# A fused attention-and-experts kernel: the beginning rebuilt (S summed in PSUM, first features on TensorE, divisors inverted once a column, chunks of up to 512 columns)

## Chip, cores and metric

The kernel runs on one core of a Trainium2 chip. The metric is the device time of one execution in microseconds (us), the median of several. Executions with a profile also give a span, from the first to the last instruction; in those used here the time is 1.75 to 2.1 us more than the span.

## The reference, cut

Polysketch attention is followed by four small experts, all weighted by gates.

```python
# q, k, v: (4 batches, 4 heads, 1088 positions, 32); S1, S2: (8, 32), double precision
def phi(x):                       # 64 features a position: products of two sketches of 8
    a, b = S1 @ x, S2 @ x
    return outer(a, b)
q_p, k_p = phi(q), phi(k)
kv  = sum over positions of k_p (x) v          # 64 x 32 for each batch and head
z   = sum over positions of k_p                # 64
num = q_p . kv;   den = q_p . z + 1e-6
x   = (num / den), as 4352 rows of 128 columns (4 heads x 32)
p   = domain_probs / (sum + 1e-9)              # (4352, 4)
out = sum over e of p[:, e] * (relu(x @ w1[e]) @ w2[e])   # w1: 128 x 1024, w2: 1024 x 128
```

## The kernel before

The experts' work runs transposed: 128 rows of x or of hidden units on the partitions, positions along the columns. Every product is done in two halves of 64 output columns of the array:

```python
def product(out, weights, moving, **flags):
    for r in (slice(0, 64), slice(64, P)):
        nc.tensor.matmul(out[r, :], weights[:, r], moving, **flags)
```

The positions go in 14 chunks of 128 to 384 columns. For each chunk there are 32 steps: `hp` = w1 part times xT, an eviction on VectorE (maximum with 0, times the gate, into `hid`), and `acc` += w2 part times `hid`. The attention of later chunks is cut into pieces; one piece is issued a step, so that it lies beside the experts. The first chunk has nothing to lie beside, and that is `start()`:

```python
kn[0] = load_rows(k, 0, "kn")
vn[0] = load_v(0, (nc.sync, nc.scalar))     # ten loads, six of them issued by ScalarE
qn[0] = load_rows(q, 0, "qn")
load_weights(0)
nc.vector.memset(warm[:, :], 0.0)
nc.scalar.activation(warm[:, 0:1], warm[:, 1:2], ACTF.Identity)   # behind ScalarE's loads
for _ in range(13):                          # the warm-up multiplications, on `warm`
    nc.tensor.matmul(wp[:, :], warm[:, 0:P], warm[:, :], start=True, stop=True)
...
def start():
    # kT; gates; q transposed; kf = k times both parts of S (high and low, side by side)
    # fs = high part copied by ScalarE, low part added by VectorE; kp = products of features
    # (VectorE and GpSimd); kv = sums over positions
    # q: one product, then shuffles, an add and multiplications on VectorE
...
def queries(b, ch):      # its end, for every chunk
    for p in range(2):
        product(nd[p][:, 0:n], kvzs[b][:, p, :], qp[p][:, 0:n], start=True, stop=True)
    # half of nd[p] holds numerators, the other half denominators, 32 equal rows a head
    for p in range(2):
        nc.scalar.activation(den[64*p : 64*p+64, 0:n], nd[p][64-64*p : 128-64*p, 0:n],
                             ACTF.Identity, bias=eps[64*p : 64*p+64, :])
    for s in range(0, n, P):
        nc.vector.reciprocal(den[:, s : s+w], den[:, s : s+w])
    for p in range(2):
        nc.vector.tensor_tensor(out=xT[r, 0:n], in0=nd[p][r, 0:n], in1=den[r, 0:n], op=ALU.mult)
```

The gates are normed on VectorE and GpSimd, transposed, stored to DRAM, and loaded again, broadcast to all partitions, one load a chunk.

Of the kernel before, what the change touches and what calls it, by code (L numbers as in the profile page):

```python
# [22 lines left out]
def kernel(  # L23
# [19 lines left out]

    nc = tc.nc

    P = 128
    B, H, S, D = q.shape
    E, DM, F = w1.shape
    R = 8
    G = S // 32  # L50
# [3 lines left out]
    NK = E * FB  # L54
    CW = 384
    GE = 160
    LA = 2
    WIDTHS = [[192, 256, 320, 320], [384, 384, 320], [384, 384, 320], [384, 384, 192, 128]]
    assert all(sum(w) == S for w in WIDTHS)

    cpool = ctx.enter_context(tc.tile_pool(name="const", bufs=1))
    lpool = ctx.enter_context(tc.tile_pool(name="loads", bufs=2))
    apool = ctx.enter_context(tc.tile_pool(name="attn", bufs=2))
    mpool = ctx.enter_context(tc.tile_pool(name="moe", bufs=2))
    ps_h = ctx.enter_context(tc.tile_pool(name="ps_h", bufs=2, space=bass.MemoryType.PSUM))
    ps_o = ctx.enter_context(tc.tile_pool(name="ps_o", bufs=2, space=bass.MemoryType.PSUM))
    ps_f = ctx.enter_context(tc.tile_pool(name="ps_f", bufs=2, space=bass.MemoryType.PSUM))
    ps_n = ctx.enter_context(tc.tile_pool(name="ps_n", bufs=2, space=bass.MemoryType.PSUM))
    dram = ctx.enter_context(tc.tile_pool(name="dram", bufs=1, space=bass.MemoryType.DRAM))
    ctx.enter_context(tc.manual_schedule())  # L70


    def load_rows(src, b, name):
        t = lpool.tile([P, S], F32, tag=name, name=name)
        nc.sync.dma_start(t[:, :], bass.AP(src.tensor, src.offset + b * H * S * D, [[G * D, P], [1, G * D]]))
        return t

    def load_v(b, engines):
        t = lpool.tile([P, H * NT * D], F32, tag="vn", name="vn")
        base = v.offset + b * H * S * D  # L80
        for r in range(2):
            for a in range(4):
                engines[r].dma_start(
                    _ap(t, 32 * a, 32, 512 * r, [[P, H], [1, P]]),
                    bass.AP(v.tensor, base + (16 * r + 4 * a) * D, [[G * D, 32], [S * D, H], [1, 4 * D]]),
                )
        for a in range(2):
            engines[1].dma_start(
                _ap(t, 32 * a, 32, 1024, [[D, H], [1, D]]),
                bass.AP(v.tensor, base + (32 + a) * D, [[G * D, 32], [S * D, H], [1, D]]),  # L90
            )
        return t

    kn, qn, vn = {}, {}, {}

# [16 lines left out]
    vn[0] = load_v(0, (nc.sync, nc.scalar))  # L112
    qn[0] = load_rows(q, 0, "qn")
    load_weights(0)
# [4 lines left out]
    nc.scalar.activation(warm[:, 0:1], warm[:, 1:2], ACTF.Identity)  # L119

    own2 = cpool.tile([P, 2], F32, name="own2")
    eps = cpool.tile([P, 1], F32, name="eps")
    sk = cpool.tile([P, P], F32, name="sk")
    sq = cpool.tile([P, P], F32, name="sq")
    nc.gpsimd.memset(sk[:, :], 0.0)
    nc.gpsimd.memset(sq[:, :], 0.0)
    nc.gpsimd.memset(own2[:, :], 0.0)
    nc.gpsimd.memset(eps[:, :], 1e-6)
# [4 lines left out]
    vx = []  # L133
    for i in range(2):
        vx.append(cpool.tile([P, NT, H, D + 1], F32, name=f"vx{i}"))
        nc.gpsimd.memset(vx[i][:, :, :, D : D + 1], 1.0)

    def product(out, weights, moving, **flags):

        for r in (slice(0, 64), slice(64, P)):  # L140
            nc.tensor.matmul(out[r, :], weights[:, r], moving, **flags)  # L141


    for _ in range(13):
        wp = ps_h.tile([P, 512], F32, tag="h", name="wp")
        nc.tensor.matmul(wp[:, :], warm[:, 0:P], warm[:, :], start=True, stop=True)  # L146

# [42 lines left out]

    R2 = 2 * R
    for h in range(H):
        (nc.vector.tensor_copy if h % 2 else nc.scalar.copy)(
            _ap(sk, 32 * h, 32, R2 * h, [[H * R2, 2], [1, R2]]), _ap(s_T, 0, 32, 0, [[D, 2], [1, R2]])
        )
        nc.gpsimd.tensor_copy(_ap(sq, 32 * h, 32, 32 * h, [[R2, 2], [1, R2]]), _ap(s_T, 0, 32, 0, [[D, 2], [1, R2]]))

    mask_lo = [R2 + l % R2 for l in range(32)]
# [13 lines left out]

    def make_gates():
# [5 lines left out]
    def store_gates():  # L219
        nc.vector.transpose(pt[:, :], pn[:, :])  # L220
        for b in range(B):
            nc.sync.dma_start(
# [4 lines left out]
    gate, xT, c0 = {}, {}, {}  # L227
    for b in range(B):
        for ch, n in enumerate(WIDTHS[b]):
            c0[b, ch] = sum(WIDTHS[b][:ch])  # L230

    def load_gate(b, ch):
        n = WIDTHS[b][ch]
        gt = mpool.tile([P, CW * E], F32, tag="gate", bufs=3, name="gate")
        nc.sync.dma_start(gt[:, 0 : n * E], gates[b, c0[b, ch] * E : (c0[b, ch] + n) * E].partition_broadcast(P))
        gate[b, ch] = gt

    ready = []
    WP = 2 * (D + 1)
# [3 lines left out]
    fss, kps = {}, {}  # L243

    def key_turn(b, r):
        if r < 2:
            nc.vector.transpose(
                _ap(kT, 0, P, 512 * r, [[32, 4], [P, 4], [1, 32]]),
                _ap(kn[b], 0, P, 512 * r, [[P, 4], [32, 4], [1, 32]]),
            )  # L250
        else:
            nc.vector.transpose(kT[:, 1024:S], kn[b][:, 1024:S])

    def value_copy(b, copy):
        ve = vx[b % 2]
        for r in range(2):
            copy(
                ve[:, 4 * r : 4 * r + 4, :, 0:D].rearrange("p t h d -> p h t d"),
                _ap(vn[b], 0, P, 512 * r, [[P, H], [D, 4], [1, D]]),
            )  # L260
        copy(ve[0:64, 8, :, 0:D], _ap(vn[b], 0, 64, 1024, [[D, H], [1, D]]))

    def key_project(b, gi):

        t0, n = FG[gi]
        if gi == 0:
            fss[b] = apool.tile([P, NT, H * R2], F32, tag="fs", name="fs")
            kps[b] = apool.tile([P, NT, 2, P], F32, tag="kp", name="kp")
        kf = ps_f.tile([P, 512], F32, tag="f", name="kf")
        for t in range(n):  # L270
            product(
                kf[:, P * t : P * t + P], kT[:, P * (t0 + t) : P * (t0 + t + 1)], sk[:, :], start=True, stop=True
            )
        nc.scalar.copy(fss[b][:, t0 : t0 + n, :], _ap(kf, 0, P, 0, [[P, n], [1, H * R2]]))  # L274
        return kf

    def key_add(b, gi, kf):
        t0, n = FG[gi]
        nc.vector.tensor_tensor(  # L279
            out=fss[b][:, t0 : t0 + n, :],  # L280
            in0=_ap(kf, 0, P, H * R2, [[P, n], [1, H * R2]]),
            in1=fss[b][:, t0 : t0 + n, :],
            op=ALU.add,
        )

    def key_product(b, t0, n, h, x, eng):
        eng.tensor_tensor(  # L287
            out=_ap(kps[b], 0, P, 256 * t0 + P * (h // 2) + 64 * x + 32 * (h % 2), [[256, n], [R, 4], [1, R]]),
            in0=_ap(fss[b], 0, P, 64 * t0 + R2 * h + 4 * x, [[64, n], [1, 4], [0, R]]),
            in1=_ap(fss[b], 0, P, 64 * t0 + R2 * h + R, [[64, n], [0, 4], [1, R]]),  # L290
# [3 lines left out]
    def key_sum(b, p, kv, heads):  # L294

        ve = vx[b % 2]
        for t in range(NT):
            n = min(P, S - P * t)
            product(
                kv[:, 256 * p : 256 * p + heads.stop * (D + 1) - heads.start * (D + 1)],  # L300
                kps[b][0:n, t, p, :],
                ve[0:n, t, heads].rearrange("p h d -> p (h d)"),
# [4 lines left out]
    def key_divide(b, kv, first_pair, step):  # L307


        kvz = apool.tile([P, 2, P], F32, tag="kvz", name="kvz")  # L310
        for off, by_pair, src, by_d in ((0, 192, 0, 1), (64, 64, D, 0)):
            nc.vector.tensor_tensor(  # L312
                out=_ap(kvz, 0, P, off, [[by_pair, 2], [D, 2], [1, D]]),
                in0=_ap(kv, 0, P, first_pair + src, [[step, 2], [D + 1, 2], [by_d, D]]),
# [5 lines left out]
    def keys(b):  # L320
# [3 lines left out]
        kf = [key_project(b, 0)]  # L324
        yield
        kf.append(key_project(b, 1))
        yield
        key_add(b, 0, kf[0])
        yield
        key_add(b, 1, kf[1])  # L330
        kf.append(key_project(b, 2))
        yield
        value_copy(b, nc.scalar.copy)
        key_add(b, 2, kf[2])
        for t0, n in ((0, 4), (4, 5)):
            for h in range(H):
                for x in range(2):
                    key_product(b, t0, n, h, x, nc.gpsimd)
        yield
        for _ in range(8):  # L340
            yield
        kv = ps_f.tile([P, 512], F32, tag="f", name="kv")
        for p in range(2):
            key_sum(b, p, kv, slice(2 * p, 2 * p + 2))
            yield
        key_divide(b, kv, 0, 256)
        yield

    kvzs = {}

    def queries(b, ch):
        n, g0 = WIDTHS[b][ch], c0[b, ch] // 32
        qT = apool.tile([P, CW], F32, tag="qT", name="qT")
        nc.vector.transpose(qT[:, 0:n], qn[b][:, 32 * g0 : 32 * g0 + n])  # L354
        yield
        yield
        qc = ps_f.tile([P, 512], F32, tag="f", name="qc")
        product(qc[:, 0:n], sq[:, :], qT[:, 0:n], start=True, stop=True)
        yield
        qf = apool.tile([P, CW], F32, tag="qf", name="qf")  # L360
# [4 lines left out]
        qb = apool.tile([P, CW], F32, tag="qb", name="qb")  # L365
        nc.vector.stream_shuffle(in_=qf[:, 0:n], out=qb[:, 0:n], mask=mask_b)
        yield
        qp = [apool.tile([P, CW], F32, tag=f"qp{p}", name=f"qp{p}") for p in range(2)]
        for x in range(2):
            qa = apool.tile([P, CW], F32, tag="qa", name="qa")  # L370
            nc.vector.stream_shuffle(in_=qf[:, 0:n], out=qa[:, 0:n], mask=mask_a[x])  # L371
            yield
            for p in range(2):
                nc.vector.tensor_tensor(  # L374
                    out=qp[p][64 * x : 64 * x + 64, 0:n],
                    in0=qa[64 * p : 64 * p + 64, 0:n],
# [193 lines left out]
```

## Time and profile before

| | before |
|---|---|
| time, median of 4 | 537.77 us (536.57 to 537.88) |
| span of the profiled execution | 534.7 us |
| TensorE busy | 518.1 us (97%) |
| VectorE busy | 333.5 us (62%) |
| first product of the experts (`hp`) | at 27.09 us |
| last product of the experts ends | at 531.1 us |

The prediction below shows the chain.

In the first 9 us TensorE does nothing, then 4.3 us of warm-up alone, then 13.8 us in which it and VectorE take turns. This is what the change is after. (The clock column reads 1.00 in the second line, although the first seven multiplications of the warm-up came every 0.43 us and the later ones every 0.21. The trace's record of the clock begins at 11.70 us only, and the column counts what lies before as full.)

### The profile page before, as it was taken

What the parts mean: (1) busy time and instruction counts of PE and PEld (TensorE: products, weight loads), DVE (VectorE), ACT (ScalarE), POOL (GpSimd) and SP (SyncE); (2) the same over time, 40 slices, a digit from 0 to 9 for tenths busy, and PEclk for the clock granted to TensorE, in tenths of its full rate; (3) what the DMA queues carried; (4) which work ended last, traced back from release to release, by engine and by line L of the source; (5) the groups of instructions that cost most, each with busy time, mean ns of one, the idle gap of its engine ahead of it and who ended that gap; (6) DMA issues with size and microseconds to landing.
All of it is one profiled execution on the core that took longest, in us unless ns stands there. A gap on an engine that the chain in (4) does not pass through costs nothing.

```text
span 534.7 us, 9910 instructions
## 1 busy us (share of the span) xinstructions
PE 518.1 (97%) x4197; PEld 287.0 (54%) x4197; DVE 333.5 (62%) x788; ACT 25.3 (5%) x56; POOL 26.1 (5%) x80
## 2 busy tenths in 40 slices
PE   3799999999999999999999999999999999999997
PEld 1677776555554445544554445454555444444896
DVE  3878874777647645367866754447875664654554
ACT  1210000000000001000000000100000000000000
POOL 2240000000000004000000000400000000000000
PEclk9999999999999999999999999999999999999999
DMA  7492502002015002000202001100301000100100
GB/s 209 109 276 103 157 28 71 0 1 73 1 49 139 2 0 77 1 1 8 67 2 63 1 0 23 53 1 0 75 1 31 12 1 10 26 1 2 16 9 8
DMA packets 32893, 22.82 MB, mean 43 GB/s; under 512 B 21200, under 2 KB 29520, under 8 KB 32848
## 3 DMA queue, kind: packets, MB, share of 16 engines
q1 hardware_dynamic: 31536, 21.78, 14.7%
q8 instruction: 33, 0.54, 0.4%
q10 hardware_dynamic: 1312, 0.40, 0.4%
q14 instruction: 12, 0.10, 0.1%
HBM read 19.87 MB, written 2.31 MB: 41 GB/s over the span
## 4 chain that ended last, share of the span: by engine, by line
PE 95%; DVE 2%; DMA 1%; issue 1%; ACT 0%; SPq 0%; DVEq 0%; ACTq 0%
PE hp L141 44%; PE acc L141 44%; PE nd L141 3%; PE kv L141 1%; PE qc L141 1%; PE kf L141 1%; PE wp L146 1%; DMA kn<-in_k_dram 1%; DVE kp L287 1%; DVE den L399 0%; DMA vn<-in_v_dram 0%; DVE qp L374 0%; DVE fs L279 0%; DVE hid L492 0%; ACT den L389 0%
## 5 line engine op out<-in xcount | busy, mean ns | idle before, releaser
L492 DVE SCALAR_TENSOR_TENSOR hid<-hp,gate 128x384 f32<-128x384 f32 (+4 forms) x448 | 213.4, 476 | 185.4 <-PE hp L141 176.8
L141 PE MATMUL hp<-xT,w_sb 128*64 128x384 f32 (+4 forms) x1792 | 311.5, 426 | 1.2 <-DVE xT L404 1.0
L141 PE MATMUL acc<-hid,w_sb 128*64 128x384 f32 (+4 forms) x1792 | 311.0, 425 | 0.0
L141 PEld LDWEIGHTS acc<-hid,w_sb 128*64 128x64 f32 x1792 | 128.6, 137 | 106.9 <-issue 68.7
L141 PEld LDWEIGHTS hp<-xT,w_sb 128*64 128x64 f32 x1792 | 126.8, 137 | 106.0 <-issue 62.6
L287 POOL TENSOR_TENSOR kp<-fs 128x128 f32<-128x128 f32 (+1 forms) x56 | 22.6, 443 | 310.9 <-DVE fs L279 310.9
L399 DVE RECIPROCAL den<-den 128x128 f32<-128x128 f32 (+1 forms) x37 | 32.3, 876 | 0.2 <-ACT den L389 0.2
L389 ACT ACTIVATE den<-nd,eps 64x384 f32<-64x384 f32 (+4 forms) x28 | 14.4, 514 | 359.3 <-issue 313.4
L374 DVE TENSOR_TENSOR qp<-qa,qb 64x384 f32<-64x384 f32 (+4 forms) x56 | 26.6, 474 | 1.3
L141 PE MATMUL nd<-qp,kvz 128*64 128x384 f32 (+4 forms) x112 | 17.6, 427 | 0.7 <-DVE kvz L312 0.7
L371 DVE STREAM_SHUFFLE qa<-qf 128x384 f32<-128x384 f32 (+4 forms) x28 | 14.0, 502 | 0.0
L404 DVE TENSOR_TENSOR xT<-nd,den 64x384 f32<-64x384 f32 (+4 forms) x28 | 13.2, 473 | 0.5
L141 PEld LDWEIGHTS kv<-vx,kp 128*64 128x64 f32 (+1 forms) x288 | 11.9, 137 | 3.0 <-issue 2.0
L141 PE MATMUL kv<-vx,kp 128*64 128x66 f32 (+3 forms) x288 | 13.0, 238 | 0.0
L146 PE MATMUL wp<-warm 128*128 128x512 bf16 x13 | 4.3, 501 | 9.0 <-ACT warm L119 9.0
L141 PEld LDWEIGHTS nd<-qp,kvz 128*64 128x64 f32 x112 | 8.0, 137 | 8.0 <-issue 4.5
L141 PE MATMUL qc<-qT,sq 128*64 128x384 f32 (+4 forms) x56 | 9.8, 426 | 1.5 <-DVE fs L279 1.5
L141 PEld LDWEIGHTS kf<-sk,kT 128*64 128x64 f32 x144 | 8.2, 137 | 3.9 <-issue 2.6
L141 PE MATMUL kf<-sk,kT 128*64 128x128 f32 x144 | 9.8, 275 | 0.5 <-DVE fs L279 0.5
L354 DVE STREAM_TRANSPOSE qT<-qn 128x384 f32<-128x384 f32 (+4 forms) x14 | 6.9, 493 | 2.9 <-DMA qn<-in_q_dram 2.9
L146 PEld LDWEIGHTS <-warm 128*128 128x128 bf16 x13 | 1.5, 124 | 11.3 <-ACT warm L119 9.0
L274 ACT COPY fs<-kf 128x256 f32<-128x256 f32 (+1 forms) x12 | 3.8, 319 | 77.5 <-PE kf L141 77.5
(59 smaller groups left out, 64.5 us busy)
## 6 DMA issues: line engine op xcount, KB each, us to landing
gate<-gates SPq DMA_DIRECT2D x6, 768.0 KB, 4.3
w_sb<-in_moe_w_dram SPq DMA_DIRECT2D x8, 512.0 KB, 8.9
gate<-gates SPq DMA_DIRECT2D x4, 640.0 KB, 4.3
kn<-in_k_dram SPq DMA_DIRECT2D x4, 544.0 KB, 4.1
qn<-in_q_dram SPq DMA_DIRECT2D x4, 544.0 KB, 3.9
vn<-in_v_dram SPq DMA_DIRECT2D x28, 64.0 KB, 3.9
out_dram<-ob SPq DMA_DIRECT2D x24, 48.0 KB, 1.8
gate<-gates SPq DMA_DIRECT2D x2, 384.0 KB, 5.4
```

The source lines that it names most:

```text
L141: nc.tensor.matmul(out[r, :], weights[:, r], moving, **flags)
L146: nc.tensor.matmul(wp[:, :], warm[:, 0:P], warm[:, :], start=True, stop=True)
L274: nc.scalar.copy(fss[b][:, t0 : t0 + n, :], _ap(kf, 0, P, 0, [[P, n], [1, H * R2]]))
L287: eng.tensor_tensor(out=_ap(kps[b], 0, P, 256 * t0 + P * (h // 2) + 64 * x + 32 * (h % 2), [[256, n], [R, 4], [1, R]]), in0=_ap(fss[b], 0, ...
L354: nc.vector.transpose(qT[:, 0:n], qn[b][:, 32 * g0 : 32 * g0 + n])
L371: nc.vector.stream_shuffle(in_=qf[:, 0:n], out=qa[:, 0:n], mask=mask_a[x])
L374: nc.vector.tensor_tensor(out=qp[p][64 * x : 64 * x + 64, 0:n], in0=qa[64 * p : 64 * p + 64, 0:n], in1=qb[64 * p : 64 * p + 64, 0:n], op=A ...
L389: nc.scalar.activation(den[64 * p : 64 * p + 64, 0:n], nd[p][64 - 64 * p : 128 - 64 * p, 0:n], ACTF.Identity, bias=eps[64 * p : 64 * p + 6 ...
L399: nc.vector.reciprocal(den[:, s : s + w], den[:, s : s + w])
L404: nc.vector.tensor_tensor(out=xT[b, ch][r, 0:n], in0=nd[p][r, 0:n], in1=den[r, 0:n], op=ALU.mult)
L492: nc.vector.scalar_tensor_tensor(out=_ap(hid[i], 0, P, 0, [[32, n // 32], [1, 32]]), in0=_ap(hp, 0, P, 0, [[32, n // 32], [1, 32]]), scala ...
```

## The change

The beginning is laid out anew, and the data with it. The parts are:

1. Warm-up and loads: the warm-up waits for a memset alone; q is loaded ahead of v; v comes in fewer, larger loads.
2. The two parts of S are summed by accumulating in PSUM. Before, they were put side by side, copied and added.
3. In the beginning the queries' features come ready from TensorE (weights `sr` hold S with its rows repeated), so no shuffles.
4. nd is arranged by kind: one tile of denominators, one of numerators. The denominators are transposed, one element of 32 is inverted, and the result is transposed back while it is broadcast.
5. Ten chunks (256, 416, 416, six of 512, and 192 columns), two steps grouped in one; VectorE makes all key products of later batches.

```diff
-    NK = E * FB
-    WIDTHS = [[192, 256, 320, 320], [384, 384, 320], [384, 384, 320], [384, 384, 192, 128]]
+    NQ = E * FB // 2
+    UNITS = [[256, 416, 416]] + [[384, 352, 352]] * 3
+    CHUNKS = [256, 416, 416] + [512] * 6 + [192]
...
     kn[0] = load_rows(k, 0, "kn")
-    vn[0] = load_v(0, (nc.sync, nc.scalar))
     qn[0] = load_rows(q, 0, "qn")
-    load_weights(0)
...
-    nc.scalar.activation(warm[:, 0:1], warm[:, 1:2], ACTF.Identity)
+    nc.scalar.activation(idle[:, :], warm[:, 0:1], ACTF.Identity)
+    vn[0] = load_v(0, (nc.sync, nc.scalar))
+    load_weights(0)
...
         for t in range(n):
-            product(kf[:, P*t : P*t+P], kT[:, P*(t0+t) : P*(t0+t+1)], sk[:, :], start=True, stop=True)
-        nc.scalar.copy(fss[b][:, t0 : t0+n, :], _ap(kf, 0, P, 0, [[P, n], [1, H*R2]]))
+            for i in range(2):
+                both(kf[:, HP*t : HP*t+HP], kT[:, P*(t0+t) : P*(t0+t+1)], sk[:, HP*i : HP*i+HP],
+                     start=(i == 0), stop=(i == 1))
...
+        fq = [psum(ps_n, "num"), psum(ps_n, "den"), psum(ps_o, "o0")]
+        for i in range(3):
+            for j in range(2):
+                both(fq[i][:, 0:n], sr[:, i, j, :], qT[:, 0:n], start=(j == 0), stop=(j == 1))
...
+        nc.sync.dma_start(w1_sb[:, 1, :], w1[1])
         store_gates()
...
-            nc.vector.reciprocal(den[:, s : s + w], den[:, s : s + w])
+        nc.vector.transpose(dT[:, 0:n], nd[0][:, 0:n])
+        nc.vector.tensor_scalar(out=rc[:, 0 : n//32], in0=_ap(dT, 0, P, 0, [[32, n//32]]),
+                                scalar1=1e-6, scalar2=1.0, op0=ALU.add, op1=ALU.mult)
+        nc.vector.reciprocal(rc[:, 0 : n//32], rc[:, 0 : n//32])
+        nc.vector.transpose(_ap(rb, 0, P, 0, [[32, n//32], [1, 32]]),
+                            _ap(rc, 0, P, 0, [[1, n//32], [0, 32]]))
```

(The cuts leave out index work and the regrouping of the steps; `both` is `product` under a new name. `hp` and `acc` are called `h` and `o` in the profiles of the kernel after, `kf` and `kv` are `f`, in the beginning also `h`.)

## The prediction

> **What bounds the kernel now.** I read the page's chain first, then the chain of waits of the first 60 us, then the groups by form.
>
> ```profile
> PE 95%; DVE 2%; DMA 1%; issue 1%; ACT 0%; SPq 0%; DVEq 0%; ACTq 0%
> PE   3799999999999999999999999999999999999997
> DVE  3878874777647645367866754447875664654554
> ```
>
> The first line (chain that ended last) gives TensorE 95% of the span; the slices show it full from the third slice to the last but one. So there are two parts: a beginning in which TensorE waits for the first columns, and a long part in which its own work is the time. The chain of waits shows where they meet:
>
> ```profile
> 1.39 3.78 DMA kn<-in_k_dram
> 5.19 2.26 DMA vn<-in_v_dram
> 7.53 1.20 issue
> 8.99 4.30 PE wp L146 x13
> 13.29 1.05 PE kf L141 x16
> ...
> 15.23 1.53 DVE kp L287 x4
> 16.76 0.46 DVE fs L279 x2
> 17.22 0.25 DVE pt L220
> 17.47 1.91 DVE kp L287 x4
> ...
> 24.38 0.42 ACT den L389
> 24.82 1.38 DVE den L399 x2
> ...
> 27.09 0.57 PE hp L141 x4
> ```
>
> Columns: start, length, what. ScalarE issues loads of v until 7.4 us, then loads its table (1.28 us), and only then may the warm-up multiplications (wp) start, at 8.99, though k has been there since 5.17. VectorE's key features, query features and two reciprocals follow, and the first product of the expert layers (hp) starts at 27.09.
>
> From there the starts of matmuls in the timeline are regular: one product (four MATMULs, two column halves) takes 325 ns for 192 columns, 432 for 256, 538 for 320, 645 for 384. That is **5 ns plus 1.667 ns a column**. All work after 27.09:
> - Experts: 4352 columns x 32 x 2 = 278,528 columns x 1.667 = 464.2, and 14 chunks x 64 = 896 products x 5 ns = 4.5: 468.7 us.
> - nd 2 x 4160 columns: 14.0. qc 4160 columns: 7.0. kf of batches 2 and 3 and one left tile: 19 x 0.218 = 4.1. kv: six groups (`kv` x36) of 1.20 us and 0.1 before the next product starts: 7.8.
>
> Sum 501.6. The last product ends at 531.13, so 504.04 passed: gaps of 2.4 us. Then a transpose, the stores and their landing: 3.6 to the end, 534.7. The measured time, 537.84, is 3.1 over the span.
>
> **What the Trainium skill says.**
> - "TensorE: Matmul & The Clock Gate", Part 1: TensorE starts at half clock, doubles after about 3.4 us of activity, and a warm matmul costs N/2.4 GHz plus about 2.5 ns. The trace agrees: wp matmuls start every 0.43 us from 8.99 to 11.84, then every 0.21; the 5 ns above are two such slots.
> - "SBUF — State Buffer", section "SBUF: two separate sides": a VectorE operation with two SBUF inputs and a GpSimd operation that reads SBUF lock one another out for whole instructions. The trace agrees in size: kp on VectorE took 442 ns for 128 elements beside GpSimd; other tensor-tensor operations of 128 took 282 to 284.
> - "DMA: Bandwidth & Descriptors", section "Issuing engines are not separate DMA queues": all DMAs share 16 engines, and a second issuing engine saves only issue time. In this trace at most 8 loads are in flight; the q load, fourth in need, is issued at 6.61 and lands at 10.22.
>
> **The change, the beginning.** I lay it out engine by engine with this trace's durations.
> - *TensorE warm-up.* wp now waits only for a memset that ends at 1.2. Fourteen take about 4.5 us: done at 5.8, beside the loads. This removes about 7 us from the front.
> - *Loads.* q is issued right after k, at 1.8, and lands near 7.
> - *Keys.* k lands at 5.2, VectorE copies four pieces of sk until 5.55, kT is ready from 6.25. kf now sums both parts of S in PSUM: 9 tiles x 2 products of 64 columns. At 64 columns the weight load sets the pace: I take kv's rate at 66 columns, 1.3 us / 9 = 0.144. 18 x 0.144 = 2.6 us, against 9 x 0.218 = 2.0 before. 6.25 to 8.85. The three VectorE adds go.
> - *Query features.* Three products of the two parts of S, 256 columns: 6 x 0.432 = 2.6 us, 8.85 to 11.45. The shuffles, the add and their chain from 19.38 to 22 go. GpSimd's weights (sr, twelve copies of about 0.29 in three sets) are ready at about 5.9, 8.2 and 9.8, each just in time.
> - *Key products.* VectorE starts after the gate transpose at about 9.0: four operations of 256 elements at 0.42 (now one input from PSUM, so no lock) and the rest, done near 11.7. GpSimd does three, 9.8 to 11.6. They lie beside TensorE now.
> - *kv.* 66 columns instead of 132: 2 x 1.3 = 2.6 against 4.8. 11.45 to 14.05. The four qp products (1.5 us) lie beside it.
> - *Division.* kvz 0.55 to 14.7; nd's denominators 0.43 + 0.25 latency: 15.4. Transpose 0.43, add 0.11, reciprocal of 8 columns 0.18 (34 columns took 367 ns, 128 took 942), transpose back 0.42, multiplication 0.42, with semaphore gaps 1.7: **first hp at 17.1**, against 27.09. It is also 256 columns instead of 192.
>
> TensorE in order, 6.25 + 2.6 + 2.6 + 2.6, sets this more than VectorE does.
>
> **The change, the long part.**
> - Experts: the same columns, 10 chunks x 64 = 640 products: 464.2 + 3.2 = 467.4 (1.3 less).
> - nd is only arranged otherwise, four half products a unit: 8192 columns, 13.8. qc 4096 columns: 6.9.
> - kf of three batches, 54 x 0.144 = 7.8 (3.7 more: a third batch is no longer hidden in the beginning, and narrow products are dearer). kv 7.8.
>
> Sum 503.7, 2.1 us **more** than before. VectorE loses the long reciprocals and 128 evictions; by row this is:
>
> ```profile
> L492 DVE SCALAR_TENSOR_TENSOR hid<-hp,gate 128x384 f32<-128x384 f32 x192 | 106.8, 556 | 117.6 <-PE hp L141 116.2
> L399 DVE RECIPROCAL den<-den 128x128 f32<-128x128 f32 x31 | 29.2, 942 | 0.2 <-ACT den L389 0.2
> L287 POOL TENSOR_TENSOR kp<-fs 128x160 f32<-128x160 f32 x28 | 12.2, 471 | 0.3 <-DVE fs L279 0.3
> ```
>
> Evictions of 256, 416, 512 and 192 columns at an estimated 0.41, 0.59, 0.69, 0.35 make 193 us for 213. Reciprocals fall from 32 to about 2, transposes for them add about 14. Almost none of it is on the path: the third number of the first row says VectorE waits for TensorE. What it can give is in the gaps of 2.4 us, of which some 1.7 lie at 40.3 to 42.9, where evictions stood behind reciprocals. I put the gaps after at 2.2, half of it start-up latency and a late gate.
>
> Total: 17.1 + 503.7 + 2.2 + 3.65 (192 columns in the tail) = 526.65, plus 3.1: **529.8 us**, 1.5% faster.
>
> **Rivals.**
> - *The gates become the wait.* The gate load must land by 17.7. Its store is issued at 9.0, behind 1.2 MB of weights still under way; at the 0.3 to 0.39 MB/us of the loads here that is over at 12.5 to 13, the store lands at 13.5, and a 512 KB broadcast lands 4 to 5 us later: 17.5 to 18.5. Here such loads took 3.0 to 7.0. Worth 0 to 3 us: 530 to 533. I count 0.5.
> - *VectorE becomes the bound in the first chunk.* 1.5 pieces of about 0.6 and two evictions of 0.41 are 1.72 a step, against TensorE's 4 x 0.432 = 1.73. Many pieces are empty or short, and two steps of lookahead cover local excess; I expect under 1 us. Later chunks have 3.4 us a step for 2.5.
> - *Wider chunks give more than 5 ns a product.* Then the long part would fall; against it: before's products show no gap at all between 384-column ones, so nothing is to be had. Only a beginning below 14.4 us would then make over 2%.
> - *The pieces run out of steps.* 68 pieces a batch against 32 a 512-column chunk is just balanced; chunk 5 needs 153 and has 152, so a wait of about half a microsecond may show there.
>
> **Range and chances.** Hand-laid beginnings err by a microsecond or two, mostly to the slow side, and the gates add up to 3; TensorE's order keeps the other side at about 527.5. Range 527.5 to 534. Over 2% faster means below 527.1, outside what the sum allows unless kf or the gaps are 2.7 us cheaper: 0.08. Slower by 2%: 0.02.
>
> **What would show it.** wp from about 1.3 us; first hp at 16.5 to 18.5; kf's 18 products in 2.6 us; hp and acc of 512 columns every 858 ns; TensorE sum after the first hp up by about 2 us; the first eviction waiting for hp, not for a gate load. The prediction is wrong if the first hp comes after 20 us, if 512-column products take over 870 ns, or if VectorE's evictions hold TensorE in the first chunk.

## More of the kernel before

One more view is worth having here, the busy time of each engine by stretch (times from the span's start; length; then TensorE's busy time with its instructions, weight loads, VectorE, ScalarE, GpSimd; granted TensorE clock; share of the DMA engines; GB/s):

```profile
0.00:9.00 9.00, 0.01 (x1) 0.01 (x1) 4.54 (x27) 1.55 (x3) 3.48 (x24) 1.00 0.65 167
9.00:13.30 4.30, 4.30 (x15) 1.58 (x17) 0.38 (x1) 0.26 (x2) 0.00 (x0) 1.00 0.90 300
13.30:27.09 13.79, 10.46 (x153) 8.58 (x153) 11.71 (x34) 3.80 (x10) 3.71 (x8) 1.00 0.43 108
```

## The result, and the profile after

The kernel after takes 528.59 us (median of 4, 528.27 to 530.55) against 537.77 us. The ratio is 0.9842 (95% interval 0.9814 to 0.9870): within 2%, and inside the range. A ratio is the mean time of one kernel's fast runs over that of the other's of the same rounds, so not quite the quotient of the medians.

Four executions have a span: 528.8 (the profiled one), 526.5, 526.5 and 527.0. So the profile shown here is of the slowest of the four, by 2 us; this matters below. Their mean granted TensorE clocks, as the record has them, are 0.996, 0.999, 1.000 and 1.000. Its chain and slices:

```profile
PE 95%; DMA 2%; DVE 1%; POOL 1%; issue 0%; DVEq 0%; SPq 0%; POOLq 0%
PE   9699999999999999999999999999999999999997
PEclk9899999999999999999999999999999999999999
```

TensorE is busy from the first slice. But the second slice has a 6 for it, and an 8 for the granted clock. The timeline of the beginning says why (start, length, engine, line, operation; in brackets the idle time before and what ended it):

```profile
1.25 5.21 PE L156 MATMUL h<-warm 128*128 128x512 bf16 x14 [1.25 <-DVE warm L131]
6.39 2.32 PE L166 MATMUL h<-sk,kT 128*64 128x64 f32 x72
11.13 2.71 PE L166 MATMUL f<-vx,kp 128*64 128x66 f32 x72
17.12 1.51 PE L166 MATMUL h<-xT,w_sb 128*64 128x256 f32 x12 [1.57 <-DVE xT L424]
20.12 0.76 DVE L531 SCALAR_TENSOR_TENSOR hid<-h,gate 128x256 f32<-128x256 f32 x2 [3.06 <-DMA gate<-gates]
20.60 0.65 PE L166 MATMUL h<-xT,w_sb 128*64 128x256 f32 x4 [1.96 <-DVE hid L531]
```

The warm-up starts at 1.25, the key features at 6.39, and the first product of the experts at 17.12, ten microseconds sooner than before. Then comes a wait that was not there before: VectorE cannot evict, as the gate has not come, and TensorE, whose three PSUM tiles are full, stands for 2 us. The chain of waits has the gate's whole way:

```profile
8.56 0.34 DVE pt L258
...
8.93 6.29 DMA gates<-pt
...
15.29 4.73 DMA gate<-gates
```

The store of the gates, 20 KB, takes 6.29 us (a median of 1.6 us before), and the load 4.73. And the clock, by stretches:

```profile
17.12:22.40 5.28, 3.03 (x22) 1.50 (x24) 1.92 (x5) 0.00 (x0) 0.00 (x0) 1.00 0.97 315
22.40:25.80 3.40, 3.40 (x20) 2.42 (x17) 1.40 (x4) 0.00 (x0) 0.00 (x0) 0.50 1.08 357
25.80:45.00 19.20, 19.20 (x174) 14.86 (x172) 14.63 (x37) 0.00 (x0) 0.00 (x0) 1.00 0.52 137
```

From 22.4 to 25.8 TensorE is granted half its clock. It is busy all of that time and does half the work, so some 1.7 us are lost. By the mean clocks above the other three executions had no such stretch, and this is most of the 2 us between them; whether the gate came late in them too, no view shows. Later there is one wait alone, at the start of a chunk:

```profile
267.70 0.55 DVE L420 STREAM_TRANSPOSE rb<-rc 128x352 f32<-128x352 f32 x1
268.28 0.53 DVE L424 TENSOR_TENSOR xT<-num,rb 128x352 f32<-128x352 f32 x1
...
268.95 1.08 PE L166 MATMUL h<-xT,w_sb 128*64 128x512 f32 x4 [0.82 <-DVE xT L424]
```

The last columns of that chunk are made only after its steps have begun. (The view gives 0.82 us, as it models the end of the multiplication before. By the starts, which come every 215 ns, the wait is 0.99 us; this number is used below.)

The sum by the prediction's own law: first `h` 17.12, TensorE's work after it 502.2 (467.4 experts, 13.8 nd, 6.9 qc, 6.3 kf, 7.8 kv), gaps 5.9, tail 3.6, together the 528.8 of the span. Of the gaps, the wait for the gate makes 2.0 us, the clock 1.7 and the wait at chunk 5 1.0.

### The profile page after: what moved, and what is told of

The parts are those of the page before. It is cut to its first block, busy times and chain, and to the rows that moved or that the text cites. A ratio compares the mean times of both kernels' runs of the same rounds, so it can differ in the third digit from the quotient of the medians.

```text
span 528.8 us, 7615 instructions
## 1 busy us (share of the span) xinstructions
PE 518.7 (98%) x3314; PEld 226.0 (43%) x3314; DVE 293.3 (55%) x628; ACT 11.3 (2%) x31; POOL 8.6 (2%) x38
## 4 chain that ended last, share of the span: by engine, by line
PE 95%; DMA 2%; DVE 1%; POOL 1%; issue 0%; DVEq 0%; SPq 0%; POOLq 0%
PE o L166 44%; PE h L166 44%; PE f L166 4%; PE den L166 1%; PE num L166 1%; DMA gates<-pt 1%; DMA gate<-gates 1%; DVE hid L531 0%; POOL sr L228 0%; DMA s_raw<-in_S_dram 0%; DVE rb L420 0%; DVE xT L424 0%; DVE qT L383 0%; DVE dT L412 0%; POOL pn L253 0%
## 5 line engine op out<-in xcount | busy, mean ns | idle before, releaser
L531 DVE SCALAR_TENSOR_TENSOR hid<-h,gate 128x512 f32<-128x512 f32 (+3 forms) x320 | 193.2, 606 | 219.3 <-PE h L166 214.5
L166 PE MATMUL h<-xT,w_sb 128*64 128x512 f32 (+3 forms) x1280 | 266.7, 530 | 4.4 <-DVE xT L424 2.4
L166 PE MATMUL o<-hid,w_sb 128*64 128x512 f32 (+3 forms) x1280 | 262.7, 530 | 0.0
L166 PEld LDWEIGHTS h<-xT,w_sb 128*64 128x64 f32 x1280 | 96.3, 138 | 138.5 <-issue 108.2
L166 PEld LDWEIGHTS o<-hid,w_sb 128*64 128x64 f32 x1280 | 96.3, 138 | 131.8 <-issue 127.1
L390 DVE TENSOR_TENSOR qp<-qa,qb 64x352 f32<-64x352 f32 (+2 forms) x44 | 23.7, 538 | 0.9
L448 DVE STREAM_SHUFFLE qa<-qf 128x352 f32<-128x352 f32 (+2 forms) x22 | 12.5, 569 | 0.0
L166 PEld LDWEIGHTS f<-vx,kp 128*64 128x64 f32 (+1 forms) x288 | 10.4, 137 | 3.8 <-issue 3.0
L166 PE MATMUL f<-vx,kp 128*64 128x66 f32 (+1 forms) x288 | 11.0, 225 | 0.0
L331 DVE TENSOR_TENSOR kp<-fs 128x256 f32<-128x256 f32 (+1 forms) x24 | 10.8, 449 | 0.0
```

Source lines behind the costliest of these rows:

```text
L166: nc.tensor.matmul(out(s), weights(s), moving(s), **flags)
L331: eng.tensor_tensor(out=_ap(kps[b], 0, P, 256 * t0 + P * p + 64 * x, [[256, n], [32, 2], [R, 4], [1, R]]), in0=in0, in1=_ap(fss[b], 0, P, ...
L390: nc.vector.tensor_tensor(out=qp[p][64 * x : 64 * x + 64, 0:n], in0=qa[64 * p : 64 * p + 64, 0:n], in1=qb[64 * p : 64 * p + 64, 0:n], op=A ...
L448: nc.vector.stream_shuffle(in_=qf[:, 0:n], out=qa[:, 0:n], mask=mask_a[x])
L531: nc.vector.scalar_tensor_tensor(out=_ap(hid[i], 0, P, CW * j, [[32, n // 32], [1, 32]]), in0=_ap(hp, 0, P, 0, [[32, n // 32], [1, 32]]), ...
```

## The experiments

My theory was that the gain comes from waits at the front, and that the shorter arithmetic adds less; that VectorE's savings elsewhere are off the path; and that a part is given back to a late gate. All twelve kernels below gave correct results. "Before" was run beside each; its medians were 537.4 to 537.9.

### What the waits alone are worth: b_warm, b_warm_q, b_front

b_warm is the kernel before with the warm-up freed of ScalarE's loads:

```diff
-    vn[0] = load_v(0, (nc.sync, nc.scalar)); qn[0] = ...; load_weights(0)     # moved down
-    nc.scalar.activation(warm[:, 0:1], warm[:, 1:2], ACTF.Identity)
+    nc.scalar.activation(idle[:, :], warm[:, 0:1], ACTF.Identity)
+    vn[0] = load_v(0, (nc.sync, nc.scalar)); qn[0] = ...; load_weights(0)
```

> The kernel before, with the warm-up matmuls freed from ScalarE's loads of v alone; q is still loaded behind v. My theory (waits at the front made most of the gain): kf starts near 6.5 instead of 13.3, but VectorE's adds stand behind the transpose of q, which lands at about 10.2, so the first hp comes about 4 us earlier (23.0) and the time falls by about 4 us to 533.7. Rival (the new arithmetic made the gain: features on TensorE, sums in PSUM): under 1.5 us of gain here.

It took 533.37 us, ratio 0.9923 (0.9907 to 0.9938): 4.1 us gained, with the first hp at 23.40. The chain (start, length, what) shows the next wait, as expected:

```profile
6.06 4.66 DMA qn<-in_q_dram
...
10.74 0.38 DVE qT L355
...
23.40 0.57 PE hp L142 x4
```

b_warm_q also loads q ahead of v:

```diff
+    qn[0] = load_rows(q, 0, "qn")      # right behind kn[0]
```

> The same, and q loaded right behind k, as in the kernel after. My theory: VectorE's adds start at about 7.8 instead of 14.8, first hp at about 20.1, time down by about 7 us to 530.8, so that only 2 to 2.5 us of the whole change is left for all its new arithmetic. Rival: under 3 us of gain, most of the 9 us needs the new arithmetic.

It took 531.97 us, 0.9897 (0.9881 to 0.9914): 5.5 us gained in all. Neither theory: the first hp came at 23.16 only. Two waits had come in the place of the old one:

```profile
2.04 5.32 DMA vn<-in_v_dram
...
8.35 1.99 PE kf L142 x16
...
15.31 4.24 DMA kn<-in_k_dram
...
19.58 1.30 DVE kT L248 x2
```

ScalarE stands until 7.4 at a small load of v, which must wait for an earlier one to land, and makes its part of sk late, so the key features start at 8.35, and at half clock (16 MATMULs in 1.99 us; they took 1.05 before). Later VectorE waits for k of batch 1 ahead of the reciprocals. b_front takes both away:

```diff
-            engines[1].dma_start(   # the last two loads of v
+            nc.sync.dma_start(
...
-        next(qs)
-        for _ in range(5):          # keys of batch 1, ahead of the first hp
-            next(ahead)
...
-        for _ in range(3):
+        for _ in range(8):          # ... and now behind it
             next(ahead)
             yield
```

> b_warm_q with two waits away that took the place of the old ones in it: the last loads of v are issued by SyncE, so that ScalarE makes its part of sk at once, and the keys of batch 1 are begun behind the first hp, so that VectorE does not wait for k of batch 1 ahead of the reciprocals. Arithmetic all as before. Theory: kf from about 6.5, first hp at about 20, 3 us earlier than in b_warm_q, while about 2 us of kf of batch 1 go to the long part: 531.0, 1 us under b_warm_q; what is left to the kernel after, 2 to 3 us, is its shorter arithmetic of the beginning. Rival: the first hp stays over 22 us, as another wait comes in.

It took 532.91 us, 0.9911 (0.9897 to 0.9924). The first hp came at 20.69, 2.5 us sooner. But nothing of it reached the end: kf of batch 1, some 2 us of TensorE's work, now lies behind the first hp, and the granted clock fell to half from 20.2 to 23.6. The mean clocks in the record show that this was no single case: 0.993 to 0.997 in the four runs of b_front, 0.996 to 1.000 in those of b_warm and b_warm_q, and 0.999 or more in every run of the kernel before. As a share of the span, that is an estimated 1.6 to 3.7 us lost in each run of b_front. So the waits alone, with the arithmetic of before, give 4 to 5.5 of the 8.5 us, by three kernels. The rest is the shorter beginning (a first hp at 17 instead of 20.7) and a clock that falls less often. These three do not show how much is which, nor which share each part of the beginning has.

### The gate: a_gate, a_gate2

a_gate moves one load of the kernel after:

```diff
-        nc.sync.dma_start(w1_sb[:, 1, :], w1[1])     # was ahead of store_gates()
...
         load_gate(0)
+        nc.sync.dma_start(w1_sb[:, 1, :], w1[1])
```

> The kernel after, with the load of w1 of expert 1 issued behind the first gate load instead of ahead of the gate stores. If the late gate is a steady cost: store lands near 13 instead of 15.2, gate near 17.5 instead of 20.0, no idle TensorE between the first three and the fourth product, time down by 1.5 to 2.5 us to about 526.5. Rival: the late gate is an accident of the one profiled run (its span was 528.8, the others' 526.5 to 527.0): under 0.5 us.

It took 528.12 us (527.52 to 528.93), ratio 0.9826 against 0.9842 for the kernel after: some 0.9 us by the ratios, between the two theories, with overlapping intervals. In its profile (span 525.7) the store landed at 14.00 and the gate at 18.67; the clock stayed full:

```profile
17.63 1.11 PE h L166 x8
18.74 0.02 issue
18.76 0.76 DVE hid L531 x2
```

a_gate2 moves the whole way forward:

```diff
-    load_weights(0)
+    nc.sync.dma_start(w1_sb[:, 0, :], w1[0])
...
-    first_factors(1)                # GpSimd: now behind pn
...
         store_gates()
+        nc.sync.dma_start(w2_sb[:, 0], w2[0]...)
...
         load_gate(0)
+        nc.sync.dma_start(w1_sb[:, 1, :], w1[1])
```

> The kernel after with the whole way of the gates moved forward: GpSimd makes pn before the second set of sr, the stores are issued behind w1 of expert 0 alone, then w2 of expert 0, the first gate load, and w1 of expert 1. If the late gate is a steady cost, the store lands near 11 to 12, the gate near 16, before the first hp at 17.1, and TensorE has no wait between the first hp and the first eviction but its own latency: 1.0 to 2.5 us under the kernel after. If it is an accident of the profiled run: within 0.5 us of a_gate and of after.

It took 527.34 us, 0.9820 (0.9803 to 0.9837): 1.2 us under the kernel after, by the ratios. The store landed at 12.59, the gate at 17.04, before the first h at 17.90. So the late gate costs about 1 us, as far as the runs can tell: the intervals overlap, but the three runs of each kernel in which the clock did not fall (see the next experiment) lie apart, at 527.07 to 527.53 us here and 528.27 to 528.77 for the kernel after, while the kernel before differed by 0.4 us between these rounds. But its profile was still of the slowest of its four runs (528.58), and no wait for the gate explains that. The clock does:

```profile
17.80:21.20 3.40, 3.30 (x16) 1.94 (x18) 1.75 (x5) 0.00 (x0) 0.00 (x0) 0.50 1.07 377
```

### The clock: a_gate2_fill

Ten multiplications of zeros go into TensorE's two waits before the first h:

```diff
+        spare = psum(ps_h, "h")
+        fill(3)                     # matmuls of the warm-up kind into spare
         rest = attend(b, 0, n, qp)
+        next(rest)                  # the denominators and numerators
+        fill(7)
```

> a_gate2 with ten idle multiplications of the warm-up kind in TensorE's two waits before the first hp (three before the denominators, seven behind them). In six of the profiles of the kernels after so far (after, a_gate_shuf, a_gate2, a_pad, a_384: yes; a_gate, a_extra: no) the granted clock fell to half for 3.4 us or 6.8 us soon after the first hp, 1.6 us lost each time. Theory: the fall comes from the idle TensorE before and after the first hp, and the fillers prevent it: clock 1.0 from 6 us to the end, the median 0.5 to 1.5 us under a_gate2 (527.3), and no runs 1.5 us above the others. Rival: the fillers only delay the first hp, or the clock falls all the same: no change or slower.

(The text names six profiles; it lists seven, five of them with a fall.) It took 527.61 us (527.27 to 527.96), 0.9811 (0.9798 to 0.9825): by the ratios 0.5 us under a_gate2, the lower end of what was expected; by the medians, of different rounds, 0.3 us over it. Neither is clear of noise. The profile had the full clock from 5.0 to the end of the work, the first h was not delayed (17.80), and the runs lay within 0.7 us, against 1.5 us for a_gate2 and 3.8 us for a_pad.

The record says more, as it has the mean clock of every run. A stretch of 3.4 us at half clock takes 0.3% off the mean, so a run at 0.997 or less had a fall. Of the 32 runs of the kernel after and its variants without fillers, 17 did. Of the 13 runs of the three kernels with fillers (this one, f_recip and a_best) none did, and each kernel's runs lay within 0.7 us of one another. b_front, run beside these three on the same chip without fillers, had a fall in four of four. So the fillers do prevent the fall. Its price, as far as single runs can tell, is 1.3 us (a_gate2: 528.58 against a mean of 527.25 for its other three) to 2.1 us (the kernel after); in runs without a fall no gain from the fillers shows.

The traces also show what decides it. In each of them the clock changes at points that are 3.41 us apart, or a multiple of it. I cut the first 36 us of all fourteen traces into stretches on that grid and took TensorE's idle time in each (the busy time of `--windows` taken off). Ahead of the eight falls the idle time was 1.76 to 2.51 us. Of the stretches at full clock that no fall followed, two had 1.80 and 1.90 us, and all others 1.66 or less. So what counts here is the sum of idle time in one stretch, with a limit near half of it, and not the longest wait (in a_gate_shuf the clock fell behind waits of at most 1.5 us, in a_gate it did not behind one of 1.6). In the profiles of the kernels with the early warm-up the grid begins anywhere from 4.1 to 6.9 us. The same two waits before the first h can therefore lie in one stretch or be divided between two, which fits a fall in some runs of one kernel and not in others.

### The rebuilt arithmetic: a_gate_shuf, f_recip

a_gate_shuf is a_gate with the first queries' features made as before:

```diff
-        fq = [...]                   # three accumulated products with sr
+        qc = psum(ps_n, "num")
+        both(qc[:, 0:n], sq[:, :], qT[:, 0:n], start=True, stop=True)
...
+        nc.vector.stream_shuffle(...)   # qf, an add, qb, and qa twice, behind the key products
```

> As a_gate, but the first features of the queries made as in the kernel before: one product with both parts of S, then shuffles and an add on VectorE. My sums: TensorE has 1.7 us less to do before kv, VectorE about 3.8 us after its key products instead of 1.7, so the first hp comes about 0.9 us later than in a_gate (18.0) and the time is 0.3 to 0.9 us over a_gate. Rival (features on TensorE are the heart of the gain): 2 us or more over a_gate.

It took 528.86 us, 0.9840 (0.9821 to 0.9859), 0.7 us over a_gate, as summed; the intervals overlap. In the profiles the first h came at 18.64 against 17.63, and the clock fell in this one. But 0.48 of that 1.01 us lies before the features: the warm-up took longer, and the key features began at 7.07 instead of 6.59. So the features on TensorE are worth about 0.5 us at the first h, and not the 2 us or more of the rival.

f_recip is a_gate2_fill with reciprocals over all elements:

```diff
-        nc.vector.transpose(dT[:, 0:n], nd[0][:, 0:n])    # ... add, reciprocal, transpose back
+        nc.scalar.activation(rb[:, 0:n], nd[0][:, 0:n], ACTF.Identity, bias=eps[:, :])
+        nc.vector.reciprocal(rb[:, 0:hn], rb[:, 0:hn])
+        yield
+        nc.vector.reciprocal(rb[:, hn:n], rb[:, hn:n])
```

> a_gate2_fill with the divisors inverted element by element as in the kernel before (an addition of eps on ScalarE, then reciprocals over all columns on VectorE, in two halves a unit), instead of once a column between two transposes. Sums: a 416-column unit costs VectorE about 2.8 us of reciprocals instead of 1.6 us, and 256 columns at the front 1.9 plus 0.5 on ScalarE instead of 1.7. Theory (VectorE is off the path after the beginning): first hp 0.6 us later, some short waits in the first chunk, 0.5 to 1.5 us over a_gate2_fill. Rival (the divisors are a main part of the gain): 3 us or more over it.

It took 529.15 us, 0.9840 (0.9826 to 0.9853) against 0.9811 (0.9798 to 0.9825): 1.5 us more. The first h came 0.86 us later (18.66), and the wait at chunk 5 grew from 0.99 to 1.90 us. In the first chunk nothing was lost. So the 30 us of reciprocals that VectorE was spared show up in two places alone, where it makes columns that TensorE already waits for.

### The long part: a_extra, a_pad, a_384

a_extra takes one piece of attention ahead of the loop (`next(pieces)` after `pieces = front()`).

> The kernel after with one piece of attention work taken ahead of the first product, so that chunk 5 finds its columns ready. The trace after has one idle of TensorE of 0.99 us at 267.5, the only one over 0.15 us after 26 us. My theory (153 pieces needed, 152 there): that idle is gone, time 1.0 us less. Rival (another wait takes its place, or it lies elsewhere in the chunk): under 0.3 us.

It took 527.95 us, 0.9828 (0.9814 to 0.9843), 0.8 us under the kernel after by the ratios, with overlapping intervals; three of its five runs had a fall of the clock, one of four for the kernel after. In its profile the wait at chunk 5 is 0.41 instead of 0.99 us: moved by one piece, it is shortened, not gone. The theory of the missing piece holds, its count was one short.

a_pad multiplies the ninth key tile with 128 rows:

```diff
-            n = min(P, S - P * t)
+            n = P
...
+    nc.gpsimd.memset(vx[HP:P, NT - 1, :, 0:D], 0.0)
```

> The kernel after with the ninth key tile multiplied at 128 rows (its lower 64 rows of key features are zero, and those of v are set to zero once) instead of 64. Theory: the two waits of 0.10 us in each kv group come from the change between 64 and 128 rows; they go, a kv group takes 1.06 us instead of 1.30, 8 groups make 1.6 to 1.9 us. Rival: they are the price of weight loads at 66 columns: no change.

As a time, 529.01 us (527.17 to 530.95), it says nothing: in its profile the gate landed at 22.11 and the clock fell twice, and by the mean clocks it fell in all five runs. The chain answers all the same. The kernel after (chain, one batch's kv groups among the experts' products):

```profile
200.79 1.20 PE f L166 x36
201.99 1.01 PE h L166 x4
203.00 1.20 PE f L166 x36
204.19 1.87 PE o L166 x8
```

and a_pad:

```profile
202.29 1.05 PE f L167 x36
203.34 0.86 PE h L167 x4
204.20 1.05 PE f L167 x36
205.25 1.72 PE o L167 x8
```

The group is 0.15 us shorter, and the product behind it no longer carries 0.15 us more (0.86 instead of 1.01, 1.72 instead of 1.87). So each group with a 64-row tile costs 0.3 us more, half of it on the 128-row product behind the group, which points to the two changes of rows. The weight loads at 66 columns cost next to nothing: without the 64-row tile a product takes 117 ns, where 5 ns plus 1.667 ns a column give 115.

a_384 has chunks of 384 columns (`[256, 416, 416] + [384] * 8 + [192]`).

> The kernel after with chunks of 384 columns instead of 512 (12 chunks instead of 10). Theory: 128 more products at 5 ns, 0.64 us more, while chunk 5's idle of 0.99 us goes, since more steps carry the same pieces: 0.3 us less than after, 0.6 us more than a_extra. Rival (wide chunks are worth more than the products' 5 ns, by fewer evictions on VectorE): 1.5 us or more over after.

It took 529.43 us (528.97 to 531.56), 0.9867 (0.9845 to 0.9889), 1.5 us over a_extra by the medians. This is more than the theory's 0.6 and does not reach the rival's size against the kernel after. But two of its five runs were 2 us over the rest, and these are the two in which the clock fell (means 0.997 and 0.996). In its profile, one of the two, the gate landed at 20.91 and the first h came at 18.11 with the same beginning. In its chain four MATMULs cost what they cost in every other kernel (a product of 384 columns 645 ns, one of 512 858 ns). Whether wide chunks are worth more than 5 ns a product stays open.

### All together: a_best

a_gate2, the fillers, two pieces ahead, and the full ninth tile.

> The kernel after with the gates' way forward, two pieces ahead (one was not enough: a_extra kept 0.41 of 0.99 us), the ninth key tile at 128 rows, and the fillers. If the parts add up: 1.0 for the pieces, 1.7 for the tile, 1 to 2 for gates and clock: 524.3 to 525.5, 2.3 to 2.5 percent under before. Rival (they hide one another): above 526.5.

It took **523.60 us** (523.52 to 523.75), ratio **0.9737** (0.9724 to 0.9751) to the kernel before: 2.6% faster, and better than the sum of parts expected. From a_gate2_fill it is 4.0 us by the medians; the wait of 0.99 us and the six groups behind the first h, at 0.3 us each, make 2.8, and 0.4 us each lie before the first h (17.39 instead of 17.80, with the other two groups) and in the first chunk, where the piece taken ahead had the queries of the next unit turned in time. The last 0.4 us I cannot place. TensorE's waits in its profile are one line, and the stretch that was half clock is whole:

```profile
PE h L157 <- DVE warm L131: 1.2, 1, 1.2
```

```profile
17.12:22.40 5.28, 5.28 (x46) 3.21 (x46) 4.33 (x13) 0.00 (x0) 0.00 (x0) 1.00 1.05 375
22.40:25.80 3.40, 3.40 (x36) 2.25 (x32) 3.23 (x10) 0.00 (x0) 0.00 (x0) 1.00 1.06 344
```

In the 3.4 us from 22.4 to 25.8 it issues 36 matmuls, where the kernel after issued 20.

## Why the prediction was right

The 529.8 us stood against 528.59. Step by step:

- **The split.** That all the gain must come from before the first product, and that the long part is TensorE's own work at 5 ns plus 1.667 ns a column, held: 512-column products came every 858 ns.
- **The beginning.** First hp predicted at 17.1, measured at 17.12. So close a hit is luck: in variants with the same beginning it was 17.4 to 18.1, and inside it errors offset one another. kf took 2.15 us instead of 2.6; from the first transpose of the denominators to the first hp it was 1.96 us instead of 1.7. The key products with one input from PSUM took 403 ns for 256 elements beside GpSimd, and those of later batches 416 without it, so no lock, as argued.
- **The warm-up.** Sized at 4.5 us, it took 5.2 and ended at 6.46 instead of 5.8. Its slow part was taken from the trace before, where it lasted 2.7 us (8.99 to 11.70), and not the 3.4 us with which the prediction says it agrees. In the kernel after it lasted 4.1 us (1.25 to 5.36), in the others with the early warm-up 2.9 to 5.7; in the profiles of the variants the warm-up ended anywhere from 5.8 to 7.2 us.
- **kf in the long part.** Sized at 144 ns a product from kv's rate; it is 116 ns, 4 ns over the law of the wide products. Together 1.5 us too much. The step that failed was "the weight load sets the pace" at 64 columns: a_pad shows that kv's slower rate comes from its 64-row tile.
- **The gate.** Named as a rival worth 0 to 3 us and counted at 0.5. The term that was too small is the store: the loads ahead of it ended at 15.07, not at 12.5 to 13, and it landed at 15.22 instead of 13.5. The landing events in the trace add that 15 of the store's 16 shares had landed by 13.96 and the last one 1.26 us later (a_pad: 15.11, and the last at 17.65); why one share came so late is open. The profiled execution lost 2.0 us to it; a_gate and a_gate2 put its mean cost near 1 us.
- **The clock.** Not foreseen at all: 1.7 us in the profiled execution, one of four of the kernel after, and a fall in 17 of the 32 runs of it and its variants without fillers.
- **Chunk 5.** The missing piece was foreseen at half a microsecond; it cost 0.99 us.
- **VectorE in the first chunk.** Foreseen as no bound; a_best shows TensorE without any wait there. (The evictions add up to 194.6 us from the durations printed, not 193; measured 193.2. Nothing rests on it.)
- **From span to time.** 3.1 us were added, from the median of before and the span of one execution that was 1.3 us faster than that median. In that same execution the difference was 1.8 us.

In the profiled execution, the offset (1.3 too much) and kf (1.5 too much) stand against gaps of 5.9 us instead of 2.2: 529.8 - 1.3 - 1.5 + 3.7 = 530.7, against 530.55 measured. So the near hit at the median is in part two errors that offset one another; the structure was right, three terms of it were not.

## What to carry to other kernels

When a trace shows one engine full after a beginning, lay the beginning out engine by engine with that trace's own durations; half of what such a rebuilding gains may be a load order and a warm-up that waits for the wrong thing. Issue a small round trip through memory that everything waits for ahead of the bulk loads; behind them it took 6.29 us here instead of 1.6. And look at the granted clock behind the short idles of TensorE in a beginning, in every run and not in one profile: here a few idle multiplications in the gaps took away a fall that cost 1.7 us.

## What the Trainium skill lacked or had wrong

- "TensorE: Matmul & The Clock Gate", section "HAM oscillation — how this bites in real kernels", gives the rule of no idle gaps over some 3.4 us. Here the clock fell to half, for 3.4 us at a time, with single idles of no more than 3.0 us (the kernel after: 0.6, 1.6 and 2.0; the longest, 3.0, in b_front). The section behind it already has short idles that make the clock swing, but no size. Here 1.76 to 2.51 us of idle time in one stretch of 3.41 us came before each of eight falls.
- No page has the rate at which narrow products follow one another with two column halves in turn. A product of 64 moving columns with four weight loads of 64 columns took 116 ns here, where 5 ns plus 1.667 ns a column, as for the wide ones, give 112. So the loads did not set the pace.
- "TensorEngine Tiling (Array Packing)", section "Key Properties", says that a change of tiling mode drains TensorE, with no price. Here a change between 128 and 64 rows and back cost 0.3 us a kv group (1.20 against 1.05 us, and 0.15 us in the product behind it).
- "DMA: Bandwidth & Descriptors", section "Anatomy of one DMA — SWDGE (gpsimd) path", has a fixed part of about 2 us for transfers that GpSimd issues. No page has what a small one costs behind others. A store of 20 KB issued by SyncE took 1.6 us with idle queues (median before) and 6.2 us behind some 1.5 MB of loads (after). A second issuing queue did not help, as the section says that the prediction cites: the two stores on ScalarE's queue took 5.4 us.
